# Round 0 of expert routing: operands of the counting matmuls swapped, its tiles in a pool of their own, fewer and moved VectorE steps

## The chip, the cores and the metric

The kernel runs on one core of one Trainium2 chip. The metric is the device time of one execution in microseconds; three executions of the kernel before gave 770.68, 771.52 and 771.63, median 771.52. TensorE is called PE here, VectorE DVE in the profile's rows, ScalarE ACT, GpSimd POOL, SyncE SP.

## The reference

Linear attention over 8 batches of 8 heads (576 positions of 64) gives 4608 tokens of 512 numbers. They go to 8 experts of exactly 576 tokens each:

```
logits = x @ w_gate                       # 4608 x 8
for idx in argsort(-logits.flatten()):    # largest logit first
    if token not assigned and counts[e] < 576: assign token to e
for e in range(8): out[mask_e] = relu(x[mask_e] @ w1[e]) @ w2[e]     # 512 -> 1024 -> 512
```

## The kernel before

**Attention** works in 16 units (a pair of batches by a pair of heads). `Plan` lists every step with an engine, a due time and dependencies, and puts each engine's steps into one fixed order, which is then issued (`manual_schedule`). The last unit (`lastu`, L302 to L307) turns its product into rows of x: VectorE makes the eight logit parts of each token (L303) and adds them to `L` (L304), ScalarE the 64 columns of each head (L307).

**Routing** runs in 8 rounds; each finds the expert that fills up first, and its 576 tokens. Of every open token the largest logit `m` is cut into six digits (`DIG`: four of 5 bits, two of 6; `KW` 32 or 64 values). For each digit, VectorE compares all 36 x 128 tokens with every threshold (`cmp`, L597), PE counts for each threshold and expert how many lie above (36 matmuls, L609, one for each column of tokens; `OH` is the one-hot row of the token's expert), VectorE makes a flag for each count of at least 576 (`fl`, L625), PE sums the flags over the thresholds with a matrix of ones (L629), VectorE takes the maximum (`ch`, L631) and subtracts it from the tokens' digits (L635). The first digit of round 0 (`part`) is counted for three quarters of the tokens inside attention already (`cmp0`, `cnt0`, `put0`; L505 to L514, layout `[128,32,9]`), and only the last nine columns come at its place. Then come the expert's number (`ei`, L656), which SP reads to start the weights' DMAs (L743, L750), the rank of each token (L662 to L672), its slot (L675 to L678), and one more one-hot product (`hh`, `hv`, `lo`, L682 to L699) that gives the tokens' numbers in the order of their slots; `idx` (L707 to L709) holds them for the gathers (L836) and, in column 5, for the last scatter of the expert. The generator yields `up`, and after it come the updates of the open tokens (L728 to L736).

**Order around round 0.** Round 0 runs up to `up` alone. Then `idle(11)` issues eleven 512-column matmuls on PE that compute nothing, and after them a second `Plan` (order `MOE['o']`, written out by hand) issues the rest: first `up` of round 0, then the first expert's steps with round 1's steps between them. Each engine's queue is in order. The first expert: GpSimd gathers rows (L836), PE transposes them (L866, L871), ScalarE makes the rounded part `xh` (L876) and VectorE the rest `xl` (L878); the weights come as `w1h` (ScalarE, L821) and `w1l` (VectorE, L824). An h group (L903) takes 12 matmuls: four each of xh with w1h, xh with w1l, xl with w1h. Then `fh` and `fl` (L916, L920), and y (L934, L949).

**Pools.** The tiles of routing (`rt`) and of the experts (`ffn`) are taken after attention's pools are released, so their memory is attention's.

Of the kernel before, what the change touches and what calls it, by code (L numbers as in the profile page):

```python
# [97 lines left out]
def attention(ctx, tc, nc, q, k, v, w_phi, w_gate, xs, L, C, xp, cfg={}, after=None, later=None, count=None, init=iter(())):  # L98
# [54 lines left out]
    def unit(u):  # L153
# [130 lines left out]
        for g,(j0,j1) in enumerate(JG):  # L284
# [31 lines left out]
        if not lastu:  # L316
            def lg(x):
                x_=T['x',u]; Lb=L[:,9*bp:9*bp+9,:]
                if hp==0: G.tensor_add(Lb,x_[:,:,0:8],x_[:,:,136:144])
                else:  # L320
                    for a in range(2): G.tensor_add(Lb,Lb,x_[:,:,136*a:136*a+8])
            add('lg','POOL',400. if hp==0 else 800.,d['num']+d['ns']+4.,lg,[('x',1)],frees=(('xb',u),))
        if u==NU-NP-1:
# [5 lines left out]
            for c in range(NB-1):  # L329
                def cp(x,c=c):  # L330
                    if c==0: T['cnt']=ps.tile([128,2,512],F32,name='g%d'%x['buf'][('g',u,'cnt')],bufs=1)[0:32,0,0:8]
                    count[1](T['cnt'],c,count[4](c),c==0,c==NB-2)
                P.add((('cnt',c),u),'PE',600.,place(('cnt',c),'PE',u,z0+d['prs']*(6+c)),cp,[(('pr',4),u)]+([(('cnt',c-1),u)] if c else []),lat=200.,mode='Z',slot=(('g',NG,('g',u,'cnt')),) if c==0 else (),ins=18)
# [47 lines left out]
def moe_consts(rp, nc, C, L, MC, cfg={}):  # L381
# [40 lines left out]
    half=rp.tile([128,1],F32,name='half'); un=rp.tile([128,NT],F32,name='un'); opn=rp.tile([128,8],F32,name='opn')  # L422
    tin=rp.tile([128,32],F32,name='tin'); eye8=rp.tile([128,8],F32,name='eye8')
    msk,Q={},{}
    dup=rp.tile([128,2,64],BF,name='dup'); dup2=rp.tile([128,2,128],BF,name='dup2'); ids=rp.tile([128,18,2,2],BF,name='ids')
    def bc(x,*shape): return x.to_broadcast([128,*shape])
# [122 lines left out]
    idp=rp.tile([128,2,NT],I32,name='idp')  # L549
    V.tensor_scalar(idp[:,0],idi,255,None,op0=OP.bitwise_and)  # L550
    V.tensor_scalar(idp[:,1],idi,~255,None,op0=OP.bitwise_and)
    V.tensor_copy(ids,idp.rearrange('p c (g i) -> p g c i',i=2))

def moe(ctx, tc, nc, L, xs, w1, w2, out, C, MC, R0, cfg={}):
# [22 lines left out]
    def routing(r):  # L577
# [3 lines left out]
        if not last:  # L581
# [4 lines left out]
            for i,(sh,bits) in enumerate(DIG):  # L586
                K=KW[i]; n=128//K; fin=i==ND-1
                part='n0' in R and i==0
                if part:
                    p=rps([K,8])  # L590
                    cnt0(R,p,NT//9-1,cmp0(R,NT//9-1),True,True)
                else:
                    cmp=S([128,NT//n,K,n],f'cmp{K}',BF,b=2)
                    cv=c.rearrange('p (g i) -> p g i',i=n)
                    g=0
                    for ck in (WC if wide else (9,))*(1 if K==32 else 2):
                        V.tensor_tensor(cmp[:,g:g+ck],cv[:,g:g+ck,None,:].to_broadcast([128,ck,K,n]),  # L597
                                        kt[i].rearrange('p (k i) -> p k i',i=n)[:,None].to_broadcast([128,ck,K,n]),op=OP.is_ge); g+=ck
# [7 lines left out]
                elif wide:  # L606
                    p=rps([K,8])
# [14 lines left out]
                if wide:  # L622
                    fl=S([K,8],f'fl{K}',BF)
# [171 lines left out]
    for r in range(E):  # L795
# [64 lines left out]
        for n_,bs in enumerate(XU):  # L860
# [116 lines left out]
def tile_kernel(ctx, tc, q, k, v, w_phi, moe_w_gate, moe_w1, moe_w2, out):  # L977
# [55 lines left out]
```

## Time and profile before

| | |
|---|---|
| median of 3 executions | 771.52 us |
| profiled execution | 767.25 us, of which 765.2 us span |
| busy | PE 734.5, PE weight loads 633.5, DVE 572.6, ACT 347.5, POOL 312.6 us |
| mean granted clock of TensorE | 0.977 |
| attention, round 0, experts | 0 to 279, 279 to 305, 305 to 765 us |

A row of the timeline gives start, duration, engine, line, operation, `out<-in`, shapes and count; in brackets, how long the engine idled before it and what ended that. Instructions of one engine overlap in the rows: a VectorE instruction may start 0.08 us before the one in front of it ends, and a matmul of 0.2 us may be followed by the next after 0.03.

### The profile page before, as it was taken

To read this page: it belongs to the slowest core of one execution; us is meant where nothing else is said; L and a number is where in the kernel's file an instruction comes from. 1 tells how busy PE (TensorE), PEld (TensorE's weight loads), DVE (VectorE), ACT (ScalarE), POOL (GpSimd) and SP (SyncE) were. 2 spreads that over 40 slices of the span, in tenths; PEclk is the share of its full clock that TensorE was granted. 3 is DMA by queue.
4 is the path that set the end of the run, shared out by engine and by line. 5 is a ranking of instruction groups with operands and counts; after the bars stand their busy time and mean duration, and the time that the engine had idled before them with its cause. 6 is when DMAs were issued, how large, how long until landed. Compare 5 with 4: busy or idle time off the path is not lost.

```text
span 765.2 us, 25311 instructions
## 1 busy us (share of the span) xinstructions
PE 734.5 (96%) x10824; PEld 633.5 (83%) x10824; DVE 572.6 (75%) x1495; ACT 347.5 (45%) x608; POOL 312.6 (41%) x336
## 2 busy tenths in 40 slices
PE   7799999999999976999999999999999999999997
PEld 4678888898889864798897897897897898898995
DVE  5799899999997977897697697697696696673410
ACT  2477777787778640433423423423423422442411
POOL 6587988998889810203203203203203103311002
PEclk9899999999999985899999999999999999999999
DMA  9999798989984031335505405505505406762401
GB/s 139 144 137 151 137 156 170 162 152 152 164 156 113 5 96 56 118 111 173 173 1 170 175 2 168 178 1 177 168 2 180 166 1 183 240 189 71 131 15 48
DMA packets 236944, 94.28 MB, mean 123 GB/s; under 512 B 185904, under 2 KB 223184, under 8 KB 236832
## 3 DMA queue, kind: packets, MB, share of 16 engines
q1 hardware_dynamic: 225552, 71.91, 42.8%
q0 software_dynamic: 6608, 20.16, 8.5%
q10 hardware_dynamic: 4672, 0.59, 0.8%
q8 instruction: 85, 1.39, 0.8%
q14 instruction: 27, 0.22, 0.1%
HBM read 72.58 MB, written 20.05 MB: 121 GB/s over the span
## 4 chain that ended last, share of the span: by engine, by line
PE 69%; issue 13%; DVE 9%; SPq 3%; POOL 2%; DMA 2%; ACT 2%; POOLq 0%; DVEq 0%
PE h L903 21%; PE y L934 18%; PE g L293 9%; PE g L185 4%; PE g L231 3%; DVE kgm L189 3%; PE y L949 3%; PE g L276 3%; SPq L122 2%; PE rps L613 1%; PE g L247 1%; DVE qgm L189 1%; DVE qgt L192 1%; PE rps L609 1%; PE g L260 1%
## 5 line engine op out<-in xcount | busy, mean ns | idle before, releaser
L964 POOL DMA_INDIRECT out_dram<-ysb,idx x40 | 39.4, 984 | 334.0 <-ACT ysb L957 328.0
L222 POOL TENSOR_TENSOR ks<-ks,kP 128x512 f32<-128x512 f32 x112 | 143.4, 1281 | 7.4 <-ACT kP L213 0.2
L903 PE MATMUL h<-xh,w1l 128*128 128x272 f32 (+3 forms) x512 | 141.1, 296 | 0.0
L903 PE MATMUL h<-xh,w1h 128*128 128x272 f32 (+3 forms) x512 | 140.8, 301 | 0.1
L916 ACT ACTIVATE fh<-h 128x272 fp32r<-128x272 f32 (+2 forms) x128 | 49.1, 385 | 135.5 <-PE h L903 127.7
L934 PE MATMUL y<-w2h,fh 128*128 128x512 f32 x256 | 101.2, 399 | 0.0
L934 PE MATMUL y<-w2l,fh 128*128 128x512 f32 x256 | 99.9, 395 | 0.0
L934 PE MATMUL y<-w2h,fl 128*128 128x512 f32 x256 | 99.3, 392 | 0.0
L903 PEld LDWEIGHTS h<-xh,w1h 128*128 128x128 f32 x512 | 95.3, 188 | 3.3 <-ACT fh L916 1.0
L903 PEld LDWEIGHTS h<-xh,w1l 128*128 128x128 f32 x512 | 96.4, 188 | 1.0
L903 PE MATMUL h<-xl,w1h 128*128 128x272 f32 (+3 forms) x512 | 92.5, 297 | 0.0
L213 ACT ACTIVATE kP<-kgt 128x768 f32<-128x768 f32 x96 | 73.9, 837 | 33.3 <-POOL kgt L201 19.1
L920 DVE SCALAR_TENSOR_TENSOR fl<-h,fh 128x272 fp32r<-128x272 f32 (+2 forms) x128 | 53.1, 417 | 38.3 <-ACT fh L916 21.9
L280 ACT ACTIVATE qP<-g 128x768 f32<-128x768 f32 x96 | 71.1, 814 | 18.4 <-PE g L276 18.3
L293 PE MATMUL g<-kz,qP 128*64 128x73 f32 x2304 | 77.5, 227 | 2.0 <-DVE kz L262 1.8
L293 PEld LDWEIGHTS g<-kz,qP 128*64 128x64 f32 x2304 | 74.8, 136 | 3.7 <-DVE kz L262 1.9
L903 PEld LDWEIGHTS h<-xl,w1h 128*128 128x128 f32 x512 | 75.9, 188 | 0.6
L231 PE MATMUL g<-kP,vi 64*64 64x256 f32 x1152 | 71.0, 377 | 0.4 <-DVE kgt L192 0.4
L957 ACT COPY ysb<-y 128x512 f32<-128x512 f32 (+1 forms) x40 | 21.8, 546 | 100.0 <-issue 61.6
L934 PEld LDWEIGHTS y<-w2l,fh 128*128 128x128 f32 x256 | 48.2, 188 | 9.1
L934 PEld LDWEIGHTS y<-w2h,fl 128*128 128x128 f32 x256 | 48.2, 188 | 8.9
L934 PEld LDWEIGHTS y<-w2h,fh 128*128 128x128 f32 x256 | 48.3, 189 | 8.2
(208 smaller groups left out, 1321.4 us busy)
## 6 DMA issues: line engine op xcount, KB each, us to landing
raww<-in_moe_w_dram SPq DMA_DIRECT2D x64, 512.0 KB, 5.1
xs<-xp SPq DMA_DIRECT2D x32, 288.0 KB, 4.7
ki<-in_k_dram SPq DMA_DIRECT2D x62, 144.0 KB, 4.9
qi<-in_q_dram SPq DMA_DIRECT2D x62, 144.0 KB, 4.7
vi<-in_v_dram SPq DMA_DIRECT2D x56, 144.0 KB, 4.3
vi<-in_v_dram POOLq DMA_DIRECT2D x8, 144.0 KB, 8.4
xl<-xd SPq DMA_DIRECT2D x4, 288.0 KB, 4.8
xd<-xg SPq DMA_DIRECT2D x4, 256.0 KB, 3.8
```

Source lines behind the costliest of these rows:

```text
L185: PE.matmul(p[64*bi:64*bi+64,a,128*(s-s0):128*(s-s0)+128],t[r,bi,s,:],C['w'][r,:],start=True,stop=True)
L189: V.tensor_reduce(m,vw(),axis=AX.X,op=OP.max,apply_absolute_value=True)
L213: for i in range(2): A.activation(o[:,:,:,128*i:128*i+128],t,AF.Exp,scale=1.0-2*i)
L222: else: G.tensor_add(ks,ks,kP[:,s])
L231: PE.matmul(p[64*a:64*a+64,i,0:256],v_[r,a,s,:],kP[r,s,a,:],start=s==0,stop=s==8,skip_group_check=True)
L280: for fh in range(2): A.activation(t[:,fh].rearrange('p i a s t -> p i (a s t)'),p,AF.Exp,scale=1.0-2*fh)
L293: PE.matmul(p[64*ab:64*ab+64,a,73*(j-j0):73*(j-j0)+73],T['qP',u,j//3][:,fh,a,ab,j%3,:],T['kz',u][:,a,fh,ab,:],start=fh==0,stop=fh==1)
L903: PE.matmul(p,ws[:,k,o:o+128],xx[:,k,o1:o2],start=n==0,stop=n==11)
L916: A.activation(hh[:,f,o1:o1+m1],p[:,0:m1],AF.Relu)
L920: V.scalar_tensor_tensor(hl[:,f,o1:o1+m1],p[:,0:m1],0.0,hh[:,f,o1:o1+m1],op0=OP.max,op1=OP.subtract)
L934: PE.matmul(p,hx[:,f,o:o+128],ws[:,f%2,:],start=n==0,stop=n==23)
L964: st=G.indirect_dma_start(out=ov,out_offset=bass.IndirectOffsetOnAxis(ap=iv,axis=0),in_=yv,in_offset=None)
```

## The change

- `rt` is opened ahead of attention and handed to `moe`.
- In the counts `OH` becomes the stationary operand and `cmp` the moving one; the result is 8 x K instead of K x 8. The flag step also writes the sum of its flags (`accum_out`), and the matmul after it takes that sum, broadcast to 128 columns, as stationary operand and a scaled 8 x 8 identity (`e8s`) as moving one.
- Comparisons at 64 values go in five pieces (4, 4, 4, 4, 2) instead of eight (1, 2, 3, 3 twice).
- The last unit's logits go into `L3`, three parts side by side, and one reduction sums them; unit 14 writes its sum there.
- Of `hv`'s two multiplies ScalarE takes one in round 0; the split of a token's number is 64 instead of 256, so that this part is one number for each partition (`pid`).
- `idx` columns 0 to 4 come from eight half-width matmuls into the right partitions and two copies. Column 5, with four matmuls of its own, moves behind `up`.
- ScalarE copies the second block of the first expert's rows in four pieces.

```diff
@@ attention, last unit
-    for a in range(2): V.tensor_mul(x_[:,j0:j1,136*a:136*a+8],p[:,a,:,64*a:64*a+8],rd[:,a].to_broadcast([128,n,8]))
-    for a in range(2): V.tensor_add(Lb,Lb,x_[:,j0:j1,136*a:136*a+8])
+    L3=C['L3'][:,j0:j1]
+    for a in range(2): V.tensor_mul(L3[:,:,:,1+a],p[:,a,:,64*a:64*a+8],rd[:,a].to_broadcast([128,n,8]))
+    V.tensor_reduce(Lb.rearrange('p j (e o) -> p j e o',o=1),L3,axis=AX.X,op=OP.add)
@@ moe_consts
-    for j in range(9): nc.tensor.matmul(p,cmp[:,:,j],R['OH'][:,9*bp+j,:],...)
+    for j in range(9): nc.tensor.matmul(p,R['OH'][:,9*bp+j,:],cmp[:,:,j],...)
+    V.tensor_copy(e8s[:,0],eye8[0:8])
+    V.tensor_tensor(e8s[:,1:ND],eye8[0:8]...,scl[0:8]...,op=OP.mult)
+    V.tensor_copy(pid,idp[:,0,0:1])
@@ moe
-    rp=ctx.enter_context(tc.tile_pool(name='rt',bufs=1))
+    rp=rt
-    WC=tuple(cfg.get('wc',(1,2,3,3)))
+    WC=(1,2,3,3); WC2=(4,4,4,4,2)
@@ routing
-    PE.matmul(p,cmp[:,t//n,:,t%n],OH[:,t,:],start=t==0,stop=t==NT-1)
+    PE.matmul(p,OH[:,t,:],cmp[:,t//n,:,t%n],start=t==0,stop=t==NT-1)
-    if part: V.scalar_tensor_tensor(fl,p,-float(cap),R['n0'],op0=OP.add,op1=OP.is_ge)
-    else: V.tensor_scalar(fl,p,float(cap),2.0**(-7*i),op0=OP.is_ge,op1=OP.mult)
+    if part: V.scalar_tensor_tensor(fl,p,-float(cap),R['n0'],op0=OP.add,op1=OP.is_ge,accum_out=da)
+    else: V.tensor_scalar(fl,p,float(cap),0.0,op0=OP.is_ge,op1=OP.add,accum_out=da)
-    p=rps([128,8]); PE.matmul(p,ones[0:K] if wide else ones,fl,start=True,stop=True)
+    p=rps([128,8])
+    if wide: PE.matmul(p,da.to_broadcast([8,128]),e8s[:,i],start=True,stop=True)
+    else: PE.matmul(p,ones,fl,start=True,stop=True)
-    V.tensor_mul(hv[:,:,:,c3,:],hh,ids[:,:,None,c3,:].to_broadcast([128,18,9,2]))
+    if c3==0 and wide: A.activation(hv[:,:,:,0,:],hh,AF.Copy,scale=pid)
+    elif c3==0: V.tensor_scalar(hv[:,:,:,0,:],hh,pid,None,op0=OP.mult)
+    else: V.tensor_mul(hv[:,:,:,1,:],hh,ids[:,:,None,1,:].to_broadcast([128,18,9,2]))
-    p=rps([128,9])
-    for j in range(4): PE.matmul(p,dup2[:,j%2],pb[:,:,j//2,j%2],start=j==0,stop=j==3)
-    V.tensor_copy(idx[0:64,0:5,0],p[0:64,0:9:2])
-    V.tensor_copy(idx[64:128,0:4,0],p[64:128,1:9:2])
-    V.tensor_scalar(idx[:,5],p[:,8:9],2.0,half,op0=OP.mult,op1=OP.add)
+    p=rps([128,5])
+    for j in range(4):
+        for o in (0,64):
+            k=5 if o==0 else 4
+            PE.matmul(p[o:o+64,0:k],dup2[:,j%2,o:o+64],pb[:,o//64:9:2,j//2,j%2],...)
+    V.tensor_copy(idx[:,0:4,0],p[:,0:4])
+    V.tensor_copy(idx[0:64,4,0:1],p[0:64,4:5])
     yield 'up'
+    if wide:
+        p=rps([128,1])
+        for j in range(4): PE.matmul(p,dup2[:,j%2],pb[:,8:9,j//2,j%2],start=j==0,stop=j==3)
+        V.tensor_scalar(idx[:,5],p,2.0,half,op0=OP.mult,op1=OP.add)
@@ first expert's rows
-    p,h,l=T['xv',r,b0,i]; A.copy(h,p)
+    p,h,l=T['xv',r,b0,i]
+    if r==0 and b0==1:
+        for k in range(4): A.copy(h[:,k],p[:,k])
+    else: A.copy(h,p)
@@ tile_kernel
+    rt = ctx.enter_context(tc.tile_pool(name='rt', bufs=1))
```

## Rows read from the trace of the kernel before

**Rows 1.** Chain that ended last, 282 to 317: start us, us, what.
```profile
282.62 0.05 DVEq L624
...
283.31 0.16 DVE fl L624
...
284.48 1.44 PE rps L609 x36
...
292.42 2.25 PE rps L609 x36
...
301.88 0.57 DVE hv L685 x2
...
305.47 1.07 POOL xg L836
...
309.49 6.42 DMA raww<-in_moe_w_dram
315.94 1.06 ACT w1h L821
```

**Rows 2.** Stretches: length, busy PE, PEld, DVE, ACT, POOL, granted clock, DMA.
```profile
283.00:299.00 16.00, 9.73 (x186) 8.88 (x186) 10.54 (x52) 0.00 (x0) 0.00 (x0) 0.50 0.17 39
...
304.00:309.00 5.00, 4.71 (x21) 1.76 (x22) 4.15 (x17) 1.99 (x2) 3.06 (x4) 0.50 0.63 193
...
310.00:311.00 1.00, 1.00 (x7) 0.55 (x6) 0.06 (x1) 0.59 (x1) 0.78 (x1) 0.97 0.87 242
```

**Rows 3.** Timeline of VectorE, last logits, 279 to 281.
```profile
279.32 0.17 DVE L297 TENSOR_SCALAR rd<-g 128x8 f32<-128x8 f32 x1 [0.83 <-PE g L293]
...
279.99 0.42 DVE L304 TENSOR_TENSOR L<-L,xp 128x32 f32<-128x32 f32 x2
280.44 0.23 DVE L433 TENSOR_REDUCE m<-L 128x9 f32<-128x72 f32 x1
```

**Rows 4.** Timeline of PE, two of the four groups of nine counts.
```profile
273.85 0.70 PE L512 MATMUL g<-OH,cmp 128*32 128x8 bf16 x9
...
282.04 0.70 PE L512 MATMUL rps<-OH,cmp 128*32 128x8 bf16 x9 [2.76 <-DVE cmp L509]
```

**Rows 5.** Groups by form, 283 to 299.3: busy us, mean ns of one, idle before.
```profile
L597 DVE TENSOR_TENSOR cmp<-cc,kt 128x384 bf16<-128x384 bf16 x14 | 4.3, 352 | 0.0
...
L625 DVE TENSOR_SCALAR fl<-rps 32x8 bf16<-32x8 f32 x3 | 0.5, 153 | 1.8 <-PE rps L609 1.8
...
L629 PEld LDWEIGHTS <-onesb 32*128 32x128 bf16 x3 | 0.3, 97 | 0.1
...
L640 DVE TENSOR_SCALAR c<-ch 128x1 f32<-128x1 f32 x1 | 0.1, 144 | 0.0
```

**Rows 6.** Timeline of PE and VectorE, 304 to 312.
```profile
304.56 0.25 PE L706 MATMUL rps<-pb,dup 128*128 128x9 bf16 x4 [0.29 <-DVE pb L704]
...
304.67 4.85 PE L576 MATMUL y<-onesb 128*128 128x512 bf16 x11
...
305.21 0.22 DVE L709 TENSOR_SCALAR idx<-rps,half 128x1 int32<-128x1 f32 x1
...
310.12 1.03 PE L576 MATMUL y<-onesb 128*128 128x512 bf16 x4
...
310.94 0.69 DVE L878 TENSOR_TENSOR xl<-h,xh 128x512 fp32r<-128x512 f32 x1 [1.99 <-ACT xh L876]
```

**Rows 7.** Timeline of ScalarE, VectorE and PE, 305 to 321.
```profile
305.55 1.99 ACT L821 CAST w1h<-raww 128x1024 fp32r<-128x1024 f32 x2 [23.60 <-DMA raww<-in_moe_w_dram]
...
314.16 1.05 ACT L821 CAST w1h<-raww 128x1024 fp32r<-128x1024 f32 x1 [1.95 <-DMA raww<-in_moe_w_dram]
...
317.30 0.76 DVE L920 SCALAR_TENSOR_TENSOR fl<-h,fh 128x256 fp32r<-128x256 f32 x2 [0.63 <-ACT fh L916]
...
319.85 0.40 ACT L916 ACTIVATE fh<-h 128x256 fp32r<-128x256 f32 x1
...
320.36 0.17 PE L629 MATMUL rps<-fl,onesb 128*128 128x8 bf16 x1 [0.95 <-DVE fl L627]
```

More of the change, by code (lines that the diff above doesn't have):

```diff
@@ L320, in lg @@
                 else:
-                    for a in range(2): G.tensor_add(Lb,Lb,x_[:,:,136*a:136*a+8])
+                    for a in range(2): G.tensor_add(C['L3'][:,:,:,0] if a and u==NU-2 else Lb,Lb,x_[:,:,136*a:136*a+8])
             add('lg','POOL',400. if hp==0 else 800.,d['num']+d['ns']+4.,lg,[('x',1)],frees=(('xb',u),))
@@ L330, in cp @@
                 def cp(x,c=c):
-                    if c==0: T['cnt']=ps.tile([128,2,512],F32,name='g%d'%x['buf'][('g',u,'cnt')],bufs=1)[0:32,0,0:8]
+                    if c==0: T['cnt']=ps.tile([128,2,512],F32,name='g%d'%x['buf'][('g',u,'cnt')],bufs=1)[0:8,0,0:32]
                     count[1](T['cnt'],c,count[4](c),c==0,c==NB-2)
@@ L422, in moe_consts @@
     half=rp.tile([128,1],F32,name='half'); un=rp.tile([128,NT],F32,name='un'); opn=rp.tile([128,8],F32,name='opn')
-    tin=rp.tile([128,32],F32,name='tin'); eye8=rp.tile([128,8],F32,name='eye8')
+    tin=rp.tile([128,32],F32,name='tin'); eye8=rp.tile([128,8],F32,name='eye8'); e8s=rp.tile([8,ND,8],BF,name='e8s')
     msk,Q={},{}
+    pid=rp.tile([128,1],F32,name='pid')
     dup=rp.tile([128,2,64],BF,name='dup'); dup2=rp.tile([128,2,128],BF,name='dup2'); ids=rp.tile([128,18,2,2],BF,name='ids')
@@ L511, in cnt0 @@
     def cnt0(R,p,bp,cmp,first,last):
-        for j in range(9): nc.tensor.matmul(p,cmp[:,:,j],R['OH'][:,9*bp+j,:],start=first and j==0,stop=last and j==8)
+        for j in range(9): nc.tensor.matmul(p,R['OH'][:,9*bp+j,:],cmp[:,:,j],start=first and j==0,stop=last and j==8)
     def put0(R,p):
-        R['n0']=rp.tile([KW[0],8],F32,name='n0'); V.tensor_scalar(R['n0'],p,-1.0,None,op0=OP.mult)
+        R['n0']=rp.tile([8,KW[0]],F32,name='n0'); V.tensor_scalar(R['n0'],p,-1.0,None,op0=OP.mult)
     def state():
         return dict(m=S([128,NT,1],'m'),dg=S([128,ND,NT],'dg',BF),sm=S([128,NT,1],'sm',BF),OH=S([128,NT,8],'OH',BF))
-    MC.extend((state,prep,(cmp0,cnt0,put0,prep0),DIG,KW,kt,kl,scl,k0,e8,ones,tri,dif,onef,msk,Q,dup,dup2,ids,half,un,opn,spacer,tin,eye8))
+    MC.extend((state,prep,(cmp0,cnt0,put0,prep0),DIG,KW,kt,kl,scl,k0,e8,ones,tri,dif,onef,msk,Q,dup,dup2,ids,half,un,opn,spacer,tin,eye8,e8s,pid))
     yield
@@ L530, in moe_consts @@
     V.tensor_reduce(eye8.rearrange('p (r o) -> p r o',o=1),ident.rearrange('p (q r) -> p r q',r=32)[:,0:8],axis=AX.X,op=OP.max)
+    V.tensor_copy(e8s[:,0],eye8[0:8])
+    V.tensor_tensor(e8s[:,1:ND],eye8[0:8][:,None,:].to_broadcast([8,ND-1,8]),scl[0:8].rearrange('p (i o) -> p i o',o=1).to_broadcast([8,ND-1,8]),op=OP.mult)
     yield
@@ L549, in moe_consts, with moe @@
     idp=rp.tile([128,2,NT],I32,name='idp')
-    V.tensor_scalar(idp[:,0],idi,255,None,op0=OP.bitwise_and)
-    V.tensor_scalar(idp[:,1],idi,~255,None,op0=OP.bitwise_and)
+    V.tensor_scalar(idp[:,0],idi,63,None,op0=OP.bitwise_and)
+    V.tensor_scalar(idp[:,1],idi,~63,None,op0=OP.bitwise_and)
+    V.tensor_copy(pid,idp[:,0,0:1])
     V.tensor_copy(ids,idp.rearrange('p c (g i) -> p g c i',i=2))
-def moe(ctx, tc, nc, L, xs, w1, w2, out, C, MC, R0, cfg={}):
+def moe(ctx, tc, nc, L, xs, w1, w2, out, C, MC, R0, rt, cfg={}):
     E,Dm,F=w1.shape
@@ L565, in mid @@
     def mid(x,t): return x[:,None,:].to_broadcast([x.shape[0],t,x.shape[1]])
-    state,prep,(cmp0,cnt0,put0,prep0),DIG,KW,kt,kl,scl,k0,e8,ones,tri,dif,onef,msk,Q,dup,dup2,ids,half,un,opn,spacer,tin,eye8=MC
+    state,prep,(cmp0,cnt0,put0,prep0),DIG,KW,kt,kl,scl,k0,e8,ones,tri,dif,onef,msk,Q,dup,dup2,ids,half,un,opn,spacer,tin,eye8,e8s,pid=MC
     ND=len(DIG)
@@ L589, in routing @@
                 if part:
-                    p=rps([K,8])
+                    p=rps([8,K])
                     cnt0(R,p,NT//9-1,cmp0(R,NT//9-1),True,True)
@@ L595, in routing @@
                     g=0
-                    for ck in (WC if wide else (9,))*(1 if K==32 else 2):
+                    for ck in ((WC if K==32 else WC2) if wide else (9,)*(1 if K==32 else 2)):
                         V.tensor_tensor(cmp[:,g:g+ck],cv[:,g:g+ck,None,:].to_broadcast([128,ck,K,n]),
@@ L606, in routing @@
                 elif wide:
-                    p=rps([K,8])
+                    p=rps([8,K])
                     for t in range(NT):
-                        PE.matmul(p,cmp[:,t//n,:,t%n],OH[:,t,:],start=t==0,stop=t==NT-1)
+                        PE.matmul(p,OH[:,t,:],cmp[:,t//n,:,t%n],start=t==0,stop=t==NT-1)
                 else:
@@ L622, in routing @@
                 if wide:
-                    fl=S([K,8],f'fl{K}',BF)
-                    if part: V.scalar_tensor_tensor(fl,p,-float(cap),R['n0'],op0=OP.add,op1=OP.is_ge)
-                    else: V.tensor_scalar(fl,p,float(cap),2.0**(-7*i),op0=OP.is_ge,op1=OP.mult)
+                    fl=S([8,K],f'fl{K}',BF); da=S([8,1],'da',BF)
+                    with nc.allow_low_precision(reason='counts up to 64'):
+                        if part: V.scalar_tensor_tensor(fl,p,-float(cap),R['n0'],op0=OP.add,op1=OP.is_ge,accum_out=da)
+                        else: V.tensor_scalar(fl,p,float(cap),0.0,op0=OP.is_ge,op1=OP.add,accum_out=da)
                 else:
@@ L704, in routing @@
             pb=S([128,9,2,2],'pb',BF); V.tensor_copy(pb,p)
-            p=rps([128,9])
-            for j in range(4): PE.matmul(p,dup2[:,j%2],pb[:,:,j//2,j%2],start=j==0,stop=j==3)
-            V.tensor_copy(idx[0:64,0:5,0],p[0:64,0:9:2])
-            V.tensor_copy(idx[64:128,0:4,0],p[64:128,1:9:2])
-            V.tensor_scalar(idx[:,5],p[:,8:9],2.0,half,op0=OP.mult,op1=OP.add)
+            p=rps([128,5])
+            for j in range(4):
+                for o in (0,64):
+                    k=5 if o==0 else 4
+                    PE.matmul(p[o:o+64,0:k],dup2[:,j%2,o:o+64],pb[:,o//64:9:2,j//2,j%2],start=j==0,stop=j==3,skip_group_check=True)
+            V.tensor_copy(idx[:,0:4,0],p[:,0:4])
+            V.tensor_copy(idx[0:64,4,0:1],p[0:64,4:5])
         else:
@@ L714, in routing @@
             d9=S([128,9,2,1],'d9',BF)
-            with nc.allow_low_precision(reason='under 256, and multiples of 256'): V.tensor_reduce(d9,pm,axis=AX.X,op=OP.add)
+            with nc.allow_low_precision(reason='under 64, and multiples of 64 up to 71 times 64'): V.tensor_reduce(d9,pm,axis=AX.X,op=OP.add)
             yield
@@ L982, in tile_kernel @@
     L = lp.tile([128, 36, 8], F32, name='L')
+    L3 = lp.tile([128, 9, 8, 3], F32, name='L3')
     C = consts(ctx, tc, nc, w_phi)
+    C['L3'] = L3
     C['xd'] = dp.tile([576, 512], F32, name='xd')
@@ L1004, in tile_kernel @@
         attention(actx, tc, nc, q, k, v, w_phi, moe_w_gate, xs, L, C, xp, ATT, after, prep, tuple(lambda *x, i=i: MC[2][i](R0, *x) for i in range(4)) + (lambda c: R0['cm'][c],), init())
-    moe(ctx, tc, nc, L, xs, moe_w1, moe_w2, out, C, MC, R0, {'lat0': 2.95, 'latr': 2.33, 'latc': 1.56, 'slack': 0.66, 'slack1': -0.2, 'pre': 0, 'warm': 44, 'wide': 1, 'latd': 0.46, 'lq': 0.96, 'lo': 0.49, 'lm': 1.69, 'lat7': 3.76, 'lgh': 1.56, 'lgx': 1.29, 'xs': 13, 'xb': 3, 'c0': 1, 'x0': 7, 'w0v': 1, 'xn': 4, 'w2o': 22, 'hc': 272, 'r1d': 1.56, 'w2s': 10, 'r1s': 0.0})
+    moe(ctx, tc, nc, L, xs, moe_w1, moe_w2, out, C, MC, R0, rt, {'lat0': 2.95, 'latr': 2.33, 'latc': 1.56, 'slack': 0.66, 'slack1': -0.2, 'pre': 0, 'warm': 44, 'wide': 1, 'latd': 0.46, 'lq': 0.96, 'lo': 0.49, 'lm': 1.69, 'lat7': 3.76, 'lgh': 1.56, 'lgx': 1.29, 'xs': 13, 'xb': 3, 'c0': 1, 'x0': 7, 'w0v': 1, 'xn': 4, 'w2o': 22, 'hc': 272, 'r1d': 1.56, 'w2s': 10, 'r1s': 0.0})
 _INS = ['q', 'k', 'v', 'w_phi', 'moe_w_gate', 'moe_w1', 'moe_w2']
```

## The prediction

> **What bounds the kernel now.** Read the stretches first. [...] Then read the chain of waits over that stretch [rows 1]: between the end of attention and the first expert there is one serial chain, VectorE and TensorE in turn. Five digits of the threshold search each go through 36 counting matmuls (1.44 us at a width of 32, 2.25 us at 64), then the slots, then the gather at 305.47, a weight DMA of 6.42 us that lands at 315.94, ScalarE's cast of it, and from 317 VectorE. So here a microsecond is a microsecond of the whole, until the first expert fills PE. Last, read the timeline of 304 to 321 [rows 6, 7]: eleven 512-column filler matmuls occupy PE for 4.85 us from 304.67, while VectorE does the bookkeeping of round 0. VectorE then idles 1.99 us before L878 and 0.63 us before L920. That is all its slack: at 320.36 PE has waited 0.95 us for VectorE's L627.
>
> **The change part by part.** Times are on that chain.
>
> *Logits.* Two dependent adds start at 279.99 and L433 follows at 280.44: 0.45 us [rows 3]. One reduction over 96 numbers replaces them; L433, 72 numbers, takes 0.23, so about 0.28 with its gap: -0.17 (bounds -0.2 to 0). The extra constants run ahead of L297, where VectorE idles 0.83 us [rows 3]; three small steps of about 0.15 fit.
>
> *The pool apart.* Ahead of the first flag (L624) the chain shows queue entries of VectorE from 282.62 to 283.31, seven steps of 0.10 us: waits that come with a tile whose memory attention used [rows 1]. The last nine counts end at 282.75 [rows 4]. With own memory the flag starts near 282.8: -0.5 (bounds -0.7 to 0). The expert's tiles still lie where attention was, and VectorE's first write to one is then the low part of the first weights (L824): I put the same 0.7 us of waits there, of which VectorE's step before (L736, issued long before it ends) hides 0.3: +0.4 (bounds 0 to 0.7).
>
> *Operands swapped in the counts.* Now 32 or 64 columns are loaded and 8 stream; then 8 are loaded and 32 or 64 stream. The load pace is (1.44-0.17)/36 = 0.035 and (2.25-0.20)/36 = 0.057 us [rows 1]. At the 0.50 clock a filler streams 512 columns in 0.43 us [rows 2, 6], so 32 columns take 0.027 and 64 take 0.053. A digit of 32 saves 0 to 0.3 us; I take 0.1, three times, because the strided read may cost as much when streamed as when loaded (0.035). A digit of 64 saves 0 to 0.15; I take 0. The nine matmuls of L512, strided wider, take 0.70 us in each of four groups [rows 4]; streaming at the clock of 1.00 they could save 0.27 each, or nothing; I take nothing.
> What the row shows is 9 loads of 32 columns at a stride of 18 bytes in about 0.06 us each, against 0.035 at a stride of 8 [rows 1, 4]. [...]
>
> *Flags.* L625 takes 0.153 us for 8 numbers [rows 5]; now 32 or 64, at 1.2 ns each (L433's 72 against these 8 [rows 3, 5]): +0.03 for four digits, +0.07 for two, +0.26. The sum output is not in this trace: between nothing and one more small step such as L640, 0.144 [rows 5]; I take 0.07, six times, +0.4. The ones of L629 were loaded ahead (0.097 [rows 5]); now the stationary operand is the flag itself, so its load stands behind VectorE: between 0.02 and 0.11 each, I take 0.05, +0.3.
> [...]
>
> *Fewer compare steps.* Eight become five at a width of 64. But the counts are PE's, not VectorE's: of the step sizes, 384 numbers take 0.352 [rows 5], and the first piece of 512 comes 0.2 later than the first of 128, while fewer stalls return 0.1: +0.05 twice. Bounds -1.1 (if PE were quicker than VectorE) to +0.4 for both.
>
> *Slots.* One of two multiplies (L685, 0.57 for two [rows 1]) goes to ScalarE, which idles 23.6 us up to 305.55 [rows 7] and needs some 0.45 us for 324 numbers (L916: 0.40 for 256), less than VectorE's next two steps: -0.25 (bounds -0.28 to +0.1). Eight half-width matmuls for four (0.25 us [rows 6]) cost 0.13 and one fewer VectorE step ahead of the gather returns as much: 0. Routing so far: -0.17 -0.5 -0.3 +0.26 +0.4 +0.3 +0.1 -0.25 = -0.15.
>
> *The step moved behind "up".* L709, now at 305.21, waits for no one. After the change it and its four matmuls are issued after the eleven fillers, so on PE's queue they stand behind them. VectorE, in order, then holds at L709 until 304.67 + 4.69 (eleven at 0.43) + 0.13 (eight matmuls earlier) + 0.25 (like L706) = 309.7: 4.5 us later [rows 6]. Behind it on VectorE's queue are all of round 0's bookkeeping, the low parts of the first weights, round 1's digits and L878. No DMA belongs to the step, POOL's gathers and SP's loads don't pass it, and its result is needed only at the end of the first expert. Cover: 1.99 before L878 and 0.63 before L920 [rows 6, 7]. So 4.5 + 0.4 - 2.0 - 0.6 = 2.3 us remain at 317.3, and PE's 0.95 at L629 is a wait for that same queue, so it absorbs nothing. Rounds 1 to 7 get a cheaper multiply (a scalar for each partition) on VectorE, beside a PE without gaps: 0. What is late next is L824 and L878: PE stops in its first h group for xl. Bounds 1.5 to 3.0.
>
> *First rows in pieces.* ScalarE copies 4 x 128 columns for one of 512; some 0.3 us more, hidden by the 1.95 us that it idles before the next weights [rows 7]. The first matmul could start 0.3 earlier, but its third operand is VectorE's: 0.
>
> Sum: -0.15 + 2.3 = +2.15 us on the profiled execution, 767.25 us (span 765.2 and 2.05 around it): 769.4. The median of the runs shown is 771.52, 4.3 us above that execution; carried over, 773.7.
>
> **The rivals.** (1) *The clock comes back inside the search.* A digit of 64 now streams 2304 columns, 1.9 of its 3.4 us, where 288 streamed before. If the granted clock rises to 1.00 there, streaming falls below VectorE's pace: 0.55 us less in each of the two digits (five pieces end after 1.6 us), 0.2 in each of the digits of 32 behind the rise, and the eleven fillers take 2.4 us (four take 1.03 at 0.97 and above [rows 2, 6]), so that VectorE's hold of 2.2 + 0.4 fits its 2.6 of slack. Then -0.15 - 1.1 - 0.4 = -1.65: 769.9, faster. Against: in 304 to 309 PE is busy 4.71 of 5.00 us, more densely than any digit will be, and the clock stays 0.50 [rows 2]. It decides if the clock is back before 304.
> (2) *The moved step holds nobody*, because its matmuls run ahead of the fillers: the routing sum alone, 771.4. For: PE could do them in 0.25 us. Against: order is as issued in every row here.
> (3) *The swap is worth more*: L512 saves 0.27 four times and the 32-wide digits all their 0.3: 1.7 less than the forecast, 772.0.
> (4) *All dear ends together* (accumulator reads 0.14, loads 0.11, the queue waits uncovered): 1.2 more, 774.9.
>
> **How the numbers follow.** Forecast 0.50 (its own range 772.2 to 775.2), rival 1 0.17, rival 2 0.13, rival 3 0.12, rival 4 0.08. A range of 770.0 to 775.6 leaves out about half of rival 1 and the tails of the others. 0.2% is 1.5 us, about what a measurement can tell: slower (over 773.1) from 0.8 of the forecast, rival 4 and a little of 3: 0.50; faster (below 770.0) from most of rival 1 and the low tails: 0.16; the rest, 0.34, within.
>
> **What would show it.** Right: L709's successor on VectorE idles some 4.5 us for a PE line right after the fillers; no queue waits ahead of the first flag; PE stalls about 2 us within its first h groups, on L878; the counting groups still take about 1.3 and 2.2 us at a clock of 0.50; a load on the chain in each flag matmul. Wrong: fillers that take 2.4 us, a digit of 64 under 3 us from one ch to the next, or VectorE going straight from the slots into the bookkeeping. The prediction fails as a whole if PE's first h matmul with xl comes no later after the gather than now.

## The result, and the profile after

The kernel after takes 764.27 us (median of 4 executions, 763.34 to 765.09), the kernel before beside it 771.58: a ratio of 0.9897, 95% interval 0.9863 to 0.9931, so 7.3 us faster. I had forecast 773.7 with a range of 770.0 to 775.6.

The profiled execution took 765.09 us, its span 763.2; the span before was 765.2. Three marks split the difference of -2.0: the last matmul of attention (L293) starts at 274.83 instead of 279.06 (-4.23); from there to the first index copy (L720, before L707) it takes 300.38 - 274.83 = 25.55 instead of 304.85 - 279.06 = 25.79 us (-0.24); and from the copy to the end 462.8 instead of 460.3 us (+2.5). So attention, whose work the diff leaves alone but for its last logits, gave the gain, and the part of which the prediction speaks lost time, as predicted. These two profiles hold 2.0 of the 7.3 us only, because the profiled execution before was 4.3 us quicker than its median; where the rest lies is answered by the profiles of the experiments, below.

Attention is ahead from its first unit on. Timeline of PE, first matmuls of L293 (called `num` here) of unit 0, before:
```profile
37.86 0.66 PE L293 MATMUL g<-kz,qP 128*64 128x73 f32 x13
```
and after:
```profile
33.22 0.60 PE L293 MATMUL g<-kz,qP 128*64 128x73 f32 x12
```
The view of waits over 7 to 38 us (in total, times, longest) says for whom VectorE waits there, before:
```profile
DVE kT L174 <- DMA ki<-in_k_dram: 6.9, 2, 4.2
```
and after:
```profile
DVE kT L174 <- DMA ki<-in_k_dram: 2.8, 1, 2.8
```
The loads are as large as before. The DMA view over 7 to 32 us (packets, MB, share of the time of 16 engines; then issues, KB, median us to landing), before:
```profile
q1 hardware_dynamic: 17777, 2.24, 82.5%
...
qi<-in_q_dram SPq DMA_DIRECT2D x8, 144.0 KB, 8.0
```
and after:
```profile
q1 hardware_dynamic: 20885, 2.78, 76.1%
...
qi<-in_q_dram SPq DMA_DIRECT2D x8, 144.0 KB, 4.5
```
In the same 25 us the queue moves more packets in less engine time: 0.825 x 16 x 25 us / 17777 = 18.6 ns a packet before, 14.6 ns after. Most of these packets carry 128 bytes, a line of 32 numbers of k or q (before, 2.24 MB / 17777 = 126 bytes on the mean). One thing about them differs: by the addresses in the two built programs, `ki` and `qi` lay 32 bytes past a multiple of 128 in each partition (the first at 40224) and now lie at a multiple (61696). The pool ahead of attention moves them by 20224 bytes, 158 times 128, which changes nothing in that respect; `L3` and the other new or wider small tiles add 1248, 9.75 times 128.

The stretches that answer to [rows 2], after (length, busy PE, PEld, DVE, ACT, POOL, granted clock, DMA):
```profile
279.00:295.00 16.00, 9.23 (x186) 8.40 (x186) 10.51 (x52) 0.00 (x0) 0.00 (x0) 0.54 0.17 39
300.00:305.00 5.00, 4.89 (x24) 2.02 (x23) 0.31 (x3) 1.99 (x2) 3.06 (x4) 0.57 0.51 154
306.00:307.00 1.00, 1.00 (x8) 0.59 (x7) 0.79 (x2) 0.26 (x1) 0.69 (x2) 1.00 0.73 59
311.10:314.50 3.40, 3.40 (x18) 3.40 (x18) 3.40 (x13) 1.31 (x3) 0.00 (x0) 0.50 0.18 62
```
The search still runs at the clock of 0.50 (the 0.54 of the first row comes from its first 1.4 us, before the clock fell at 280.4). The last row is new: the clock came back at 304.3 and was at 0.50 once more for 3.4 us, with PE busy throughout.

The search itself. Timeline of VectorE, after, last logits and first digit:
```profile
275.86 0.25 DVE L305 TENSOR_REDUCE L<-L 128x32 f32<-128x96 f32 x1
276.15 0.23 DVE L435 TENSOR_REDUCE m<-L 128x9 f32<-128x72 f32 x1
...
278.60 0.18 DVE L630 SCALAR_TENSOR_TENSOR fl<-rps,n 8x32 bf16<-8x32 f32 x1 [0.22 <-PE rps L514]
278.72 0.07 DVE L630 DVE_READ_ACCUMULATOR fl<-rps,n 8x1 bf16 x1
```
The first flag comes 278.60 - 274.83 = 3.77 us after attention's last matmul, where it was 283.31 - 279.06 = 4.25 [rows 1]: the queue waits ahead of it are gone, and PE's L514 is what it waits for. The chain that ended last, after, gives the last nine counts of the first digit and the 36 counting matmuls at a width of 32 and of 64:
```profile
277.78 0.72 PE rps L514 x9
...
279.83 1.39 PE rps L614 x36
...
287.99 2.09 PE rps L614 x36
```
They were 0.70 [rows 4], 1.44 and 2.25 [rows 1]. The groups by form, 279 to 295 us (busy us, mean ns of one, idle before), show what the flags cost in return:
```profile
L631 DVE TENSOR_SCALAR_CACHE_REDUCE fl<-rps 8x32 bf16<-8x32 f32 x3 | 0.5, 179 | 1.7 <-PE rps L614 1.7
L636 PEld LDWEIGHTS <-da 8*128 8x128 bf16 x5 | 0.5, 100 | 2.2 <-DVE fl L631 2.2
L631 DVE TENSOR_SCALAR_CACHE_REDUCE fl<-rps 8x64 bf16<-8x64 f32 x2 | 0.4, 212 | 1.9 <-PE rps L614 1.9
...
L631 DVE DVE_READ_ACCUMULATOR fl<-rps 8x1 bf16 x5 | 0.4, 73 | 0.0
```
From the first L639 (`ch`) to the sixth it takes 15.13 us, before 14.84 (L631). VectorE behind the slots, after:
```profile
300.38 0.16 DVE L720 CAST idx<-rps 128x4 int32<-128x4 f32 x1 [0.47 <-PE rps L719]
...
304.91 0.22 DVE L743 TENSOR_SCALAR idx<-rps,half 128x1 int32<-128x1 f32 x1 [4.30 <-PE rps L742]
...
307.13 0.69 DVE L840 TENSOR_TENSOR w1l<-raww,w1h 128x512 fp32r<-128x512 f32 x1 [0.31 <-issue]
...
308.97 0.68 DVE L897 TENSOR_TENSOR xl<-h,xh 128x512 fp32r<-128x512 f32 x1
```
That is the forecast hold: L743 stands for 4.30 us (4.5 forecast) behind the fillers. The queue waits that left the first flag now stand ahead of L840: seven queue entries 0.10 us apart, from 306.45 to 307.04.

### The profile page after: what moved, and what is told of

It is laid out like the page before. It is cut to its first block, busy times and chain, and to the rows that moved or that the text cites. A ratio compares the mean times of both kernels' runs of the same rounds, so it can differ in the third digit from the quotient of the medians.

```text
span 763.2 us, 25319 instructions
## 1 busy us (share of the span) xinstructions
PE 736.1 (96%) x10832; PEld 633.3 (83%) x10832; DVE 571.4 (75%) x1495; ACT 348.2 (46%) x612; POOL 312.0 (41%) x336
## 3 DMA queue, kind: packets, MB, share of 16 engines
q8 instruction: 85, 1.39, 0.8%
## 4 chain that ended last, share of the span: by engine, by line
PE 65%; issue 13%; DVE 12%; POOL 4%; ACT 2%; SPq 2%; DMA 1%; POOLq 0%; DVEq 0%
PE h L922 22%; PE y L953 18%; PE g L293 8%; DVE kgm L189 4%; PE y L968 3%; PE g L185 3%; PE g L276 2%; PE g L231 2%; SPq L122 2%; DVE qgt L192 2%; DVE qgm L189 2%; PE rps L618 2%; POOL ks L222 1%; PE g L247 1%; PE h L887 1%
## 5 line engine op out<-in xcount | busy, mean ns | idle before, releaser
L293 PE MATMUL g<-kz,qP 128*64 128x73 f32 x2304 | 78.9, 229 | 2.0 <-DVE kz L262 1.8
L293 PEld LDWEIGHTS g<-kz,qP 128*64 128x64 f32 x2304 | 76.3, 138 | 3.8 <-DVE kz L262 1.9
```

The lines of the kernel that those rows point to most:

```text
L293: PE.matmul(p[64*ab:64*ab+64,a,73*(j-j0):73*(j-j0)+73],T['qP',u,j//3][:,fh,a,ab,j%3,:],T['kz',u][:,a,fh,ab,:],start=fh==0,stop=fh==1)
```

## The experiments

Theory A: `ki` and `qi` at a multiple of 128 bytes take the loads faster. Rivals: the pool's place by itself, chance at the start, and, for the stretch behind the search, the hold (H) against weights that land late (R). Three medians of the kernel before, beside the runs, are 770.78 (e1 to e4), 770.69 (e5 to e8) and 771.02 (e9 to e12).

**Where the tiles lie.** e1, e2 and e5 put pads around `ki` and `qi`; e13 is e2 with 24 numbers instead of 8 in `pad0`.
```diff
+    V.memset(sb.tile([128,8],F32,name='pad0',bufs=1),0.0)   # e5, e13: 24
     for nm,x in (('k',k),('q',q)): loadx(nm,x,0,(nc.sync,nc.scalar))
+    V.memset(sb.tile([128,8],F32,name='pad1',bufs=1),0.0)
```


> Kernel before, with one thing changed: the tiles into which k and q are loaded begin 32 bytes further on, at a multiple of 64 bytes (before they lie 32 past one); v's tiles keep their place modulo 64. Theory A (place of the load targets): the 128-byte packets of k and q are what attention waits for at the start, and they take 18.9 ns each in the first 40 us of the kernel before against 14.2 ns in the kernel after, because of that place. Then they take about 14.2 ns here, unit 0's first num matmul (37.86 us before) starts at 33.2 to 33.6, and the time falls by about 4.3 us, to 767.3. Rival B (the routing pool opened ahead of attention is the cause by itself): no change, 771.6, packets 18.9 ns. Rival C (chance from execution to execution at the start): times scattered between the two, no change of the median.

Measured: 770.03, ratio 0.9994 (0.9971 to 1.0017); unit 0's matmul at 39.35. A multiple of 64 is not enough, so the first form of A fell. The two pads and their VectorE steps by themselves win nothing either.

> Kernel after, with k's and q's load tiles put back 32 bytes past a multiple of 64 by a 32-byte pad (a second pad behind them keeps all other tiles at their place modulo 64). Theory A (place of the load targets): packets of 128 bytes rise to 18.9 ns in the first 40 us, unit 0's num matmul from 33.22 to about 37.8 us, the time from 764.3 to about 768.5. Rivals B (pool) and C (chance): 764.3 as the kernel after, packets 14.2 ns.

Measured: 771.92, ratio to the kernel before 1.0009 (0.9990 to 1.0027): the whole gain is gone with the place of these two kinds of tiles. Its PE timeline and DMA view over 7 to 32 us:
```profile
39.77 0.54 PE L295 MATMUL g<-kz,qP 128*64 128x73 f32 x10
```
```profile
q1 hardware_dynamic: 15668, 1.98, 77.8%
```
That is 19.9 ns a packet.

> Kernel before, with k's and q's load tiles alone moved from 32 past a multiple of 64 bytes to a multiple of 128 (a pad of 96 bytes ahead of them; all other tiles keep their place modulo 128). In the runs so far the packets of 128 bytes took 14.0 to 14.2 ns in the first 40 us where these tiles lie at a multiple of 128 (the kernel after, and it with v moved), and 18.2 to 20.6 ns at 32 or 64 past one. Theory A' (a packet of 128 bytes is quick only if it falls on a whole multiple of 128): packets at about 14 ns, unit 0's first num matmul at 33 us, its last one at about 274.9 (279.06 before), and the time 7 us below the kernel before, 763.5 to 764.5, since the kernel after with the tiles put back lost 7.6. Rival D (what the change moved together with the tiles, such as the pool's place above them): no change, 770.8, packets at 18 ns or more.

Measured: 764.51, ratio 0.9929 (0.9905 to 0.9953). The kernel before with nothing but the place changed is as fast as the kernel after (764.27). Its PE timeline, waits over 7 to 38 us and DMA view over 7 to 32 us (13.7 ns a packet):
```profile
32.12 0.67 PE L295 MATMUL g<-kz,qP 128*64 128x73 f32 x14
```
```profile
DVE kT L176 <- DMA ki<-in_k_dram: 1.9, 1, 1.9
```
```profile
q1 hardware_dynamic: 21942, 3.06, 75.4%
```

The pool alone, in the kernel before:
```diff
+    rt = ctx.enter_context(tc.tile_pool(name='rt', bufs=1))   # ahead of attention, handed to moe
-    rp=ctx.enter_context(tc.tile_pool(name='rt',bufs=1))
+    rp=rt
```


> Kernel before, with the routing pool alone opened ahead of attention (nothing else of the change); k's and q's tiles still lie 32 past a multiple of 64, v's at a multiple. Theory A: attention as before (num of unit 0 at 37.9 us, packets 18.9 ns); only the six queue waits ahead of the first flag go (0.45 us) and return at VectorE's first tile of an expert (0.4): 771.2 to 771.6. Rival B: the 4.3 us of the start come with the pool, 767.3. Rival C: 771.6 with wide scatter.

Measured: 774.01, ratio 1.0035 (1.0015 to 1.0055): the pool by itself is slower, so this rival fell. Attention starts as before (37.95). It also shows that late loads cost beyond the start: between units 12 and 13 it loses 2.3 us, and the view of waits over 231 to 249 us names the load:
```profile
DVE qT L174 <- DMA qi<-in_q_dram: 3.2, 1, 3.2
```
The kernel before has no such wait there in its profile. Its timed executions range from 767.53 to 775.52 (29 of them), those of the kernel after from 762.96 to 765.66 (4, and 6 of e9).

The profiles of all sixteen kernels show where the rest of the 7.3 us lies. With `ki` and `qi` off a multiple of 128 (the kernel before, e1, e2, e4, e13) the last matmul of attention starts at 279.06 to 282.77 us, the kernel before's own being the earliest; with them at one (the other eleven) at 272.95 to 275.02. In e5 it starts at 273.18, 5.9 us earlier than in the kernel before.

v's tiles, and the boundary: e3 and e14 have a pad behind `qi` only, of 8 and 40 numbers.

> Kernel after, with one 32-byte pad behind q's tiles: k and q stay at a multiple of 64, and v's tiles, which the change moved 32 past one, lie at a multiple again. Theory A: v's 256-byte packets fall from about 20 ns to 18.5 or less; v is not what unit 0 waits for last, so the time falls by 0 to 1 us, 763.3 to 764.3. If v's load ends a wait of the first two units, up to 2 us. Rivals B and C: 764.3, packets of 256 bytes at 20 ns.

Measured: 763.70, ratio 0.9899 (0.9867 to 0.9931): v's packets 18.0 ns, no time won that can be told.

> Kernel after, k's and q's load tiles 96 bytes past a multiple of 128 instead of at one. If every place but a multiple of 128 costs the same, since a packet of 128 bytes then lies across two lines of 128: packets of 128 bytes at 18 to 20.6 ns in the first 40 us and 14.0 to 14.4 between 100 and 268, as at 32 and 64 past one, and unit 0's first num matmul at 38 to 40 us. If it is the size of the overlap that counts: 32 and 96 alike, 64 dearest. [...]

> Kernel after with v's tiles at a multiple of 256 bytes (k and q lie at one as in the kernel after). v's packets of 256 bytes took 19.3 to 20.6 ns at 96 past a multiple of 128, and 17.8 to 18.4 at a multiple of 128 that is not one of 256 (three kernels with quick k and q packets, 40 to 268 us). If lines of 128 are what counts: 17.8 to 18.4 here too. If a line of 256 counts as well: 14 to 16 here, each packet in one line instead of two. The time as in the kernel with v at a multiple of 128 (763.7) within 1 us either way.

Measured: 771.45 and 764.20, one execution each, beside a kernel before at 771.80. Means of the packet records, ns, by the bytes past a multiple of 128 (e14's v at one of 256):
```
k, q at      kernel                 128 B, 0-40 us   128 B, 100-268 us   unit 0's num at
32           before, e2, e4         18.9 19.6 18.2   14.0 14.3 13.9      37.86 39.77 37.95
64           e1                     20.6             14.3                39.35
96           e13                    21.1             13.9                39.50
0            after, e3, e5, e14     14.2 14.0 13.5 13.7   13.1 12.9 12.9 12.9   33.22 32.87 32.12 32.89
v at         kernel                 256 B, 40-268 us
96           after, e9              19.8 20.0
0 (not 256)  e3, e10, e12           18.0 18.3 18.1
0 (of 256)   e5, e14                17.9 17.9
```
So, of the places tried, a multiple of 128 is what counts. These are means: in the first 40 us most packets take 13 ns at 0 and at 32 alike, and what changes is the share that takes more than 20 ns, 2 to 10% at a multiple of 128 and 25 to 40% off it. Why the place does that is not shown. In the first 40 us 96 is the dearest (21.1, one execution), but from 100 us on 32, 64 and 96 are alike (13.9 to 14.3). v takes the same at a multiple of 128 (18.0 to 18.3) and at one of 256 (17.9).

**Behind the search.** The stretch from the start of attention's last matmul to the end: before 486.1, after 488.4.
```diff
 # e6: column 5's four matmuls behind the copies of columns 0 to 4, VectorE's step left
+                p5=rps([128,1])
+                for j in range(4): PE.matmul(p5,dup2[:,j%2],pb[:,8:9,j//2,j%2],start=j==0,stop=j==3)
 # e7: GpSimd's copy of the expert number, SyncE's register load and the loads of w1's
 #     third and fourth quarter go behind the first gather instead of the second; e8: both
 ...
```


> Kernel after, with the four matmuls of index column 5 issued ahead of the eleven filler matmuls, VectorE's step on it left where it is: VectorE's wait of 4.3 us (25.78 to 30.08 us after the last num matmul) goes. Theory H (this wait is what lengthens the stretch from the last num matmul to the end by 2.2 us, 488.4 against 486.1): the stretch falls to about 486.1 and the time to 762.0. Theory R (the third and fourth quarter of the first expert's w1 land late, ScalarE's casts of them start 35.4 and 38.5 us after the last num matmul against 35.1 and 36.9 before, and end the stretch by themselves; the kernel before with only the pool moved has no such wait of VectorE and is 2.2 us longer all the same): the stretch stays at 488.3, the time at 764.3.

> Kernel after, with GpSimd's copy of the expert number and SyncE's two weight loads that hang on it moved from behind the second gather to behind the first, some 1.3 us earlier; VectorE's wait for column 5 stays. Theory R: the weights land before the casts need them, the fourth quarter's cast starts at 36.9 us or earlier after the last num matmul, and the stretch to the end falls from 488.4 to 486.2 to 487, the time to 762 to 763; if the gathers behind them are delayed as much, nothing is won. Theory H: the wait of VectorE ends the stretch, 488.4, time 764.3.

> Kernel after with both: column 5's matmuls ahead of the fillers, and the two weight loads behind the first gather. Theory H: as with the first edit alone, 762.0. Theory R: as with the second alone, 762 to 763. If each of the two covers the other (either one alone keeps the stretch at 488.4), only this kernel is quicker: stretch 486.1 or less, time 762.0 or less.

Measured: 765.93 (762.85 to 767.76), 764.58 and 763.27; stretches 486.7, 487.1 and 487.7. All three are shorter than 488.4, but e8, with both edits, is longer than either alone. The earlier loads of e7 do land earlier: ScalarE's casts of them start 33.9 and 36.0 us after attention's last matmul, 36.0 and 37.5 in e9 below. In exchange PE waits for gathered rows ahead of its second group of transposes, 1.0 us in e7 and 1.7 in e8. The medians tell none of the three from the kernel after. Inconclusive without the kernel after beside them, hence e9 and the combinations (e10: e3 and e8; e12: e3 and e6).

> The kernel after, unchanged, again beside the next three: if start-up and end are the kernel's own and not chance, the last num matmul starts at 274 to 275.5 us, VectorE waits 4.2 to 4.4 us for column 5, the stretch from the last num matmul to the end is 488.2 to 488.4, and the time 764.3 +- 0.5. If the 488.4 of its first profile came from the dip of the clock at 311 to 314.5 us alone, a profile without that dip has 486 to 487.

> Kernel after with all three edits that seemed to help: v's tiles at a multiple of 128, column 5's matmuls ahead of the fillers, the weight loads behind the first gather. If the gains of the profiles hold (stretch to the end 486.7 to 487.7 instead of 488.3, v's packets 18.0 instead of 19.5 ns): 762.2 to 763.2. If the end is set by something that takes back what the two edits of the tail give: 763.7 as with v alone.

> Kernel after with v's tiles at a multiple of 128 and column 5's matmuls ahead of the fillers, the weight loads left. The same edit without v's place gave a stretch of 486.7 in its profile but timed runs from 762.9 to 767.8. If the hold is what costs in the tail: 762.0 to 763.0. If a weight load behind the fourth gather sets the end in most executions, 764 to 766, with a granted clock of 0.975 where the quick ones have 0.98.

Measured: e9 764.14, e10 763.76, e12 763.57 (ratios 0.9916, 0.9913, 0.9906, intervals about +-0.0018): the same within what can be told. None beats the kernel after for certain; e10 is its second case, e12 lies between its two. Stretches 487.3, 487.2 and 486.9; e9's, and its hold of 3.85, are below what was expected. In e9's profile the clock comes back at 302.9 and stays (columns as in the stretches above):
```profile
303.00:306.00 3.00, 2.41 (x16) 1.22 (x14) 1.75 (x8) 0.59 (x1) 2.53 (x4) 1.00 0.70 175
306.00:312.00 6.00, 4.91 (x36) 4.26 (x36) 5.88 (x22) 1.97 (x6) 1.39 (x3) 1.00 0.79 273
```
That goes with about 1 us: of the kernels with the hold, four profiles have 27.3 us at 0.50 in the search and behind it, the very end left out (the kernel after, e2, e3, e13), and stretches of 488.2 to 488.5, three have 23.9 us (e7, e9, e14), and 487.1 to 487.6. It doesn't explain the difference to the kernel before, whose profile also has 27.3 us at 0.50 (282.8 to 310.1), like e1's, and stretches of 486.1 and 486.0. e9 still holds VectorE, e12 doesn't; e9, then e12:
```profile
303.96 0.22 DVE L743 TENSOR_SCALAR idx<-rps,half 128x1 int32<-128x1 f32 x1 [3.85 <-PE rps L742]
```
```profile
299.51 0.22 DVE L746 TENSOR_SCALAR idx<-rps,half 128x1 int32<-128x1 f32 x1
```
The hold is gone, 3.85 us of it, and the stretch is 0.46 shorter (e6 against e9: 0.64 shorter; e8 against e7, the same step: 0.60 longer). Most of the hold falls where VectorE would have waited anyway; its timeline without the hold, e12:
```profile
305.07 0.69 DVE L900 TENSOR_TENSOR xl<-h,xh 128x512 fp32r<-128x512 f32 x1 [1.44 <-ACT xh L898]
...
307.18 0.69 DVE L900 TENSOR_TENSOR xl<-h,xh 128x512 fp32r<-128x512 f32 x1 [0.84 <-ACT xh L897]
...
312.44 0.76 DVE L942 SCALAR_TENSOR_TENSOR fl<-h,fh 128x256 fp32r<-128x256 f32 x2 [0.82 <-ACT fh L938]
```
That is 3.10 us, and none of it is left in e9. What PE waits for, 305 to 320 us of e9:
```profile
PE h L922 <- DVE xl L897: 1.1, 1, 1.1
...
PE rps L637 <- DVE fl L633: 0.5, 1, 0.5
```
and 304.5 to 319.5 us of e12:
```profile
PE rps L638 <- DVE fl L634: 1.0, 1, 1.0
```
With the hold PE waits 1.1 us for VectorE's `xl` and then 0.5 at the matmul of round 1's flags; without it, it waits for VectorE at that matmul alone, 1.0.

Pool and place together, in the kernel before:

> Kernel before with the pool opened ahead of attention and k's and q's load tiles at a multiple of 128: the place and the pool, and nothing else of the change (old counts, old flags, column 5 ahead of the fillers). Attention as in the kernel before with the place alone (last num matmul at 273 to 274.5), first flag 0.45 earlier. If the 2.2 us that the pool alone added behind the search belong to it (the first gather comes 0.9 us after its index column instead of 0.6, the two weight loads are issued 0.6 later and land behind the fourth gather): stretch 488.3, time 766.3. If they were chance of that execution: stretch 485.7, time 764.1. If the rest of the change is worth what I forecast for it without the hold (0.3 us slower), this kernel is at 764.0 and the kernel after without the hold at 764.3 or below.

Measured: 765.33, ratio 0.9937 (0.9917 to 0.9957). Between the two cases of the expectation, and its profile doesn't decide: the clock is back at 0.50 from 315.0 to 321.8 and the stretch 489.7; e5's, with no pool, has the same (315.1 to 322.0) and 489.1. So beside e5, with the clock alike, the pool costs 0.6 us of the stretch.

In e4 the pool's price is larger. ScalarE's casts of w1's third and fourth quarter there:
```profile
318.92 1.05 ACT L821 CAST w1h<-raww 128x1024 fp32r<-128x1024 f32 x1 [3.04 <-DMA raww<-in_moe_w_dram]
321.48 1.05 ACT L821 CAST w1h<-raww 128x1024 fp32r<-128x1024 f32 x1 [1.50 <-DMA raww<-in_moe_w_dram]
```
From the last matmul of attention (282.77) that is 36.15 and 38.71, before 35.10 (314.16 [rows 7]) and 36.88; in the kernel after 35.41 and 38.54. e4's stretch is 488.3 with no hold at all, 2.2 more than the kernel before's, at the same 27.3 us of the clock at 0.50. The pool's price thus comes out at 0.6 and at 2.2 us in two pairs of single profiles. Why these loads, issued within 0.6 us of the old place, land up to 1.8 later stays open. Early loads are no cure: e7 issued them 1.3 earlier and its stretch (487.1) is e9's within 0.2.

## Why the prediction was wrong

*The step that failed is "The pool apart": the sum has no term for attention.* The step priced seven queue waits (-0.5) and where they go (+0.4). It took the pool for a thing between routing and the experts, asked only who had used its memory before, and did not ask which tiles lie behind it: all of attention's. Attention's time was thereby put at nothing, without a reason. Together with the new and wider small tiles (`L3`, `e8s`, `pid`, `n0` and the flags) the pool set k's and q's load tiles from 32 past a multiple of 128 to a multiple. That was worth -6.2 us in the kernel before (e5), +7.6 when undone in the kernel after (e2), and it had no term and no rival. The trace before could not show the effect of a place it did not have, but the wait was there to be read: VectorE waiting 6.9 us for `ki` in a stretch that the prediction never opened. All the signs that the prediction named lie in round 0, and most of the right ones came (the hold, no queue waits ahead of the flag, counts of 1.39 and 2.09 at 0.50, PE's stop for `xl`, 1.1 instead of 2 us), so none of them could show the miss.

*Queue waits.* Right: the first flag 0.48 earlier (0.46 in e4 with the pool alone). On the other side only VectorE's L840 was priced. GpSimd's first write to an expert's tile is later too: the first gather starts 301.47 - 300.38 = 1.09 after the index copy, timeline of GpSimd after,
```profile
301.47 1.06 POOL L852 DMA_INDIRECT xg<-xs,idx  x1 [2.63 <-DMA raww<-in_moe_w_dram]
```
where it was 305.47 - 304.85 = 0.62 [rows 1]. It is 1.08 to 1.35 in every kernel with the pool ahead, e4 and e11 with the old index copies among them, and 0.62 in the others.

*Logits, swap, flags, compare pieces.* Logits -0.06 (forecast -0.17): the reduction with its gap takes 0.29 (I gave it 0.28), but it starts 0.33 after the multiplies' start, where the first add started after 0.23. The counts fell by 0.05 three times and 0.16 twice: -0.47 (forecast -0.3), so the wide digits gained as well. A flag takes 0.179 and 0.212 instead of 0.153 [rows 5], within 0.02 of the forecast, plus a read-out. The rows show the read-out as a second instruction (`DVE_READ_ACCUMULATOR`), and it takes 0.073, as I took it (0.07). The load that now stands behind VectorE takes 0.100. From the flag to `ch` it is 0.47 and 0.50 us instead of 0.41 and 0.42, so flag, read-out and load together cost 0.06 to 0.08 a digit, under half of what I had put there (0.15 and 0.19). The digits lost 0.29 in all (14.84 to 15.13); forecast: +0.3 +0.4 +0.26 -0.3 + 0.1, so +0.76. Right in sign, but for another reason: a digit of 32 takes 2.65 us as before, and the loss is in the two of 64 (3.59 instead of 3.46), whose counts start 0.48 after the first compare instead of 0.29, after a first piece of 0.418 us instead of 0.224. Here I had allowed 0.05 each.

*Slots.* From the sixth `ch` to the index copy 6.20 us instead of 6.30: -0.10 (forecast -0.25).

*The moved step.* Right in mechanism and in the length of the hold (4.30 in one profile, 3.85 in the other; forecast 4.5), too dear in its price. Of the 2.3 forecast, 4.5 less 2.6, so 1.9, were the hold's; taking it away shortened the stretch by 0.5 and 0.6 in two pairs of profiles and lengthened it by 0.6 in a third, and no median shows it. Two terms were off by the rows of e9 and e12. The cover was 3.10, not 2.6. And PE's 0.95 at round 1's flag matmul did absorb something: with the hold it is 0.5, because PE itself comes later by its 1.1 us for `xl`.

*The 2.5 us behind the index copy* can't be split for certain. The clock is not the difference (27.3 us at 0.50 in both profiles); the hold is 0.5 to 0.6 where it shows, the pool 0.6 or 2.2. That the whole stretch is 2.25 us longer in these two profiles, where 2.15 had been forecast, is luck: e4 has the same 2.2 with no hold, on which nearly the whole forecast rested.

*The rest as a whole.* Without the place the change is +1.1 us by medians (e2 against the kernel before, interval -0.8 to +2.1), and with the place on both sides -0.2 to -0.4 (e9 and the first runs against e5). The forecast of +2.15 is too dear by one to two and a half, and that the change without the place is slower at all is not shown. The test that I named for the failure of the whole, an `h` matmul with `xl` no later after the gather, did not strike: `xl` comes 308.97 - 301.47 = 7.5 us after the first gather's issue, 310.94 - 305.47 = 5.5 before [rows 1, 6].

*The rivals.* (1) did not happen: in no profile is the clock back inside the search (in the kernel after it is at 0.50 from 280.4 to 304.3, and the sixth `ch` comes at 294.19). (2) did not happen: VectorE is held (4.30), but the hold costs little, for the reasons above. (3) did not happen: L514 takes 0.72 where it took 0.70, and a digit of 32 saves 0.05 in its counts. Of (4) the loads came nearly as dear as feared (0.100 for 0.11), but the whole step from flag to `ch` did not.

## What to carry to other kernels

A new tile, or a pool opened earlier, moves the tiles behind it (here k's and q's, by 1248 and 20224 bytes): compare the addresses of DMA targets before and after, modulo 128, before pricing any instruction. Where packets are as short as these (128 bytes), put the targets at a multiple of 128 bytes; a pad of 96 bytes gave the kernel before 6.2 of the 7.3 us. And when a wait is moved onto an engine, count every place behind it where that engine would have waited anyway, and what the delay of the next engine gives back.

## What was not expected of the hardware

- A packet of 128 bytes into SBUF took on the mean 13.5 to 14.8 ns at a multiple of 128 and 18.2 to 21.1 off it while several queues load (0 to 40 us), 12.9 to 13.3 against 13.9 to 14.3 later. One of 256 bytes, beside quick ones of k and q, took 17.9 to 18.3 at a multiple of 128 and 19.4 to 20.0 at 96 past one.
- The granted clock behind the search differs between executions of one kernel: in the kernel after it came back at 304.3 and fell to 0.50 again for 3.4 us, or came back at 302.9 and stayed (e9), and the stretch differed by 1.1 us.
- An output of a sum (`accum_out`) shows as a second VectorE instruction of 0.073 us that starts before the first one ends (278.72, the first from 278.60 to 278.78).
